# Attention and MoE kernel: batch 0's second round as fp32 products on unsplit q, k and v

## The chip, the cores and the metric

The kernel runs on one core of a Trainium2 chip. The metric is the device time of one execution in microseconds (us); the times before are the median and the spread of three runs, and the profile is one further execution of the same program. The engines are named as the profile names them: PE (matmuls), PEld (its weight loads), DVE (vector), ACT (scalar), POOL (GpSimd), SP (the engine that issues the DMAs).

## The reference

Eight batches of eight heads, 576 tokens, head dimension 64; then a two-layer network with 512 model columns and 2048 inner columns.

```python
scores = (1 / sqrt(64)) * (q @ k.T)                 # (8, 8, 576, 576)
thresh = max(scores, axis=-1) - tau
scores = where(scores >= thresh, scores, -1e9)
attn = exp(scores - max(scores))
attn = attn / (sum(attn) + 1e-9)
x = (attn @ v), heads joined                        # (4608, 512)
h = x @ w_in                                        # (4608, 2048)
out = (h * sigmoid(h)) @ w_out                      # (4608, 512)
```

Inputs and outputs are fp32, and w_in and w_out come as 64-bit words that the kernel decodes itself.

## The kernel before, in words

**Tiles and visits.** The work is a list of score tiles. A tile is 128 query rows against all 576 keys of a head. Tiles are grouped in visits, a visit being one pair of heads of one batch (`visits`, L653). Batches 1 to 7 have one visit for each pair, with nine tiles. Batch 0 is done in two rounds: four visits of kind "low" (query tokens 0 to 255, four tiles each, 16 tiles), a gap of 12 empty places, then four visits of kind "high" (tokens 256 to 575, five tiles each, 20 tiles). In a high visit the third tile is mixed: 64 rows of the one head and 64 of the other. The empty places give the network of batch 0's first 256 tokens room to begin.

**A split tile** (batch 0's high round and all later batches). `load_qk` (L322) loads q and k of a head twice, into both halves of the partitions. `split_k` (L357) rounds k to the fp32r form on ACT and takes the rest on POOL (L362). `split_q` (L336) scales q by 0.125 (`gate`) and does the same; for batch 0 the scaling and the rounding are two ACT instructions (L345, L346) and the rest is POOL's (L347), for later batches ACT does it in one (L351) and DVE takes the rest (L352). `scores` (L428) makes the tile in a PSUM buffer of two halves, with rounded k and rest of k: four products, eight for a mixed tile (L448). `soft1` takes the row maximum on DVE (L458, L461), `soft1b` the exponential on ACT (L468), `soft2` masks, sums and inverts on DVE (L477, L481, L485), `soft2b` divides each row by its sum on ACT (L495), `soft3` (L499) splits the rows into two fp16 parts: the first by ACT for tiles before EARLY = 36 (L504), else by POOL (L506), the second by POOL (L509, L512). A DMA transposes both into `wT` (L522). `av` (L527) multiplies with v, which `split_v` (L308) has split into two fp16 parts on ACT and DVE (L312, L313): 28 products for a pair and column range (L537).

**A direct tile** (batch 0's low round). `load_direct` (L374) loads k of both heads once, and q of each head into its own half of a buffer whose other half is zero (`qzero`, part of `gbuf`). `scale_direct` (L382) scales q on ACT (L385). Scores are two fp32 products (L436), `soft2b` divides on POOL (L491), `soft3_direct` (L387) transposes the fp32 rows on PE (L393, L395) and ACT copies them out (L403, L404), `av_direct` (L406) multiplies with the raw v (L413).

**Weights.** `load_weights`, `decode_weights` (L184: ACT L191, DVE L194 and L197, then a product on PE, L209, that gathers the maxima in PSUM bank 2) and `split_weights` (L216) run over 16 tiles of w_in, then 16 of w_out. w_in is scaled on POOL (L226), rounded to fp16 on ACT (L229), and POOL takes the rest (L230). w_out is scaled and rounded on ACT (L221) and DVE takes the rest (L222). `W_PLAN` (L39) gives the places at which they are due; w_out's steps carry a priority offset of 150.

**The network.** `h_unit` (L573) is 12 products (L580) and then work on ACT and DVE (L588, L589, L595, L596), `o_unit` (L604) 12 products (L611). Batch 0's units are let in at RATES = 1.3, then 0.8 units for each place of the list, once the x of their tokens is there.

**PSUM.** Score buffers take four of eight banks; `bank` (L78) hands out three (m0, m1, m2, where m2 is left out of the turn until the high round's end), `ps_a` is one bank for the products with v.

**Order.** The loop at L763 writes the work down place by place; `at` puts steps at places of the list; `pri` gives some of them a priority. A planner then orders each engine's and each queue's instructions by priority and its own simulated times. On the chip every engine and the DMA queue on SP work through their own list in that order.

Of the kernel before, what the change touches and what calls it, by code (L numbers as in the profile page):

```python
# [19 lines left out]
P = 128  # L20
# [12 lines left out]
EARLY = 36  # L33
GAP, GAP1 = 12, 1
V_SLOT = 26
# [17 lines left out]
def attention_moe(  # L53
# [41 lines left out]


# [119 lines left out]
    def split_weights(i):  # L216
# [3 lines left out]
        if i >= 4 * NK:  # L220
            nc.scalar.activation(hi, w, AF.Copy, scale=sc)  # L221
            nc.vector.scalar_tensor_tensor(  # L222
                out=w16[:, i, 512:1024], in0=w, scalar=sc, in1=hi, op0=ALU.mult, op1=ALU.subtract
            )
            return
# [110 lines left out]
    def split_q(h, tiles):  # L336
# [7 lines left out]
        if h < H:  # L344
            nc.scalar.activation(src, src, AF.Copy, scale=gate)  # L345
            nc.scalar.activation(dst, src, AF.Copy)  # L346
            nc.gpsimd.tensor_tensor(  # L347
                out=dst[D:P, :], in0=src[D:P, :], in1=dst[D:P, :].bitcast(F32), op=ALU.subtract
            )
        else:  # L350
            nc.scalar.activation(dst, src, AF.Copy, scale=gate)  # L351
            nc.vector.scalar_tensor_tensor(  # L352
                out=dst[D:P, :], in0=src[D:P, :], scalar=gate[D:P, :],
                in1=dst[D:P, :].bitcast(F32), op0=ALU.mult, op1=ALU.subtract,
            )
# [11 lines left out]
    qzero = []  # L367
    for i in range(2):
        t = gbuf.bitcast(F32)[:, 4096 + 512 * i : 4608 + 512 * i]
        nc.gpsimd.memset(t, 0.0)  # L370
        qzero.append(t)

    def load_direct(v):
        b, p, _ = visits[v]  # L374
        kt = sb.tile([P, S], F32, tag="kraw", name=f"kd_{v}", bufs=2)
        nc.sync.dma_start(out=kt, in_=kT[b, 2 * p : 2 * p + 2].rearrange("h d s -> (h d) s"))
        qt = qzero[v % 2]
        nc.sync.dma_start(out=qt[0:D, 0:256], in_=qT[b, 2 * p, :, 0:256])
        nc.sync.dma_start(out=qt[D:P, 256:512], in_=qT[b, 2 * p + 1, :, 320:S])
        direct[v] = qt, kt  # L380

    def scale_direct(v):  # L382
        for j in range(2):
            own = direct[v][0][j * D : (j + 1) * D, 256 * j : 256 * (j + 1)]
            nc.scalar.activation(own, own, AF.Copy, scale=gate[j * D : (j + 1) * D, :])  # L385

    def soft3_direct(t):  # L387
# [3 lines left out]
        main = bank([P, 4, P], f"tm_{t}")  # L391
        for k in range(4):
            nc.tensor.transpose(main[:, k, :], w[:, k * P : (k + 1) * P], ident)  # L393
        last = bank([P, P], f"tl_{t}")
# [58 lines left out]
    def soft1(t):  # L453
# [6 lines left out]
        )  # L460
        nc.vector.tensor_scalar(  # L461
            out=sm[:, 1:2], in0=negm, scalar1=-1.0, scalar2=ntau, op0=ALU.mult, op1=ALU.add
        )
        small[t] = sm
        wtile[t] = w

# [295 lines left out]
    t = 0  # L762
# [93 lines left out]
```

## Time and profile before

| | |
|---|---|
| runs shown, median (lowest to highest) | 1234.36 us (1231.63 to 1234.51) |
| profiled execution, its own time | 1228.56 us |
| its span | 1226.8 us |
| granted PE clock over the span | 0.971 |
| busy: PE | 1145.4 us, 93% |
| busy: DVE | 934.2 us, 76% |
| busy: ACT | 808.6 us, 66% |
| busy: POOL | 739.4 us, 60% |

A page of the profile cuts the span in 40 slices and gives for each, in tenths, how busy an engine was and what clock PE was granted. Groups of instructions stand as line, engine, operation, output and inputs, count, then busy time in us and mean duration in ns, then the idle time of the engine just before them and who ended it. The order of time gives start, duration, engine and line. Shares over the whole span hide stages with different limits, so views of single stretches matter more here.

### The profile page before, as it was taken

How to read it: one execution, taken by the hardware profiler on the slowest of the kernel's cores; microseconds unless marked ns; L12 is line 12 of the kernel's file. 1: busy time of each engine (PE TensorE's matmuls, PEld its weight loads, DVE VectorE, ACT ScalarE, POOL GpSimd, SP SyncE). 2: the span in 40 equal slices, each digit the busy share in tenths (PEclk: the TensorE clock that was granted, in tenths of full speed). 3: DMA queues.
4: the chain of work that ended last, by engine and by line, in shares of the span. 5: the costliest groups of instructions: out<-in, count | busy, mean ns of one | idle time of the engine just before them, and what ended most of it. 6: DMA issues, size and time to landing. Idle time of an engine off the chain costs nothing.

```text
span 1226.8 us, 26991 instructions
## 1 busy us (share of the span) xinstructions
PE 1145.4 (93%) x9422; PEld 898.1 (73%) x9422; DVE 934.2 (76%) x2619; ACT 808.6 (66%) x1491; POOL 739.4 (60%) x936
## 2 busy tenths in 40 slices
PE   6867679999799999999999999999999999999998
PEld 4545458777677777877777877787778877777777
DVE  6988998987888988988889958887789848332330
ACT  5768876776777767776777747776678747333331
POOL 2289968786778778886888528872778447100000
PEclk9967889999999999999999999999999999999999
DMA  9659658687677777786896447872797346200000
GB/s 296 192 182 235 136 117 171 146 139 148 138 145 144 166 148 145 147 160 149 146 174 141 110 115 138 156 144 82 137 159 150 75 86 113 50 11 15 16 11 25
DMA packets 363480, 158.16 MB, mean 129 GB/s; under 512 B 329552, under 2 KB 338256, under 8 KB 363344
## 3 DMA queue, kind: packets, MB, share of 16 engines
q1 hardware_dynamic: 363344, 156.43, 60.6%
q8 instruction: 75, 1.23, 0.4%
q14 instruction: 61, 0.50, 0.1%
HBM read 66.72 MB, written 9.44 MB: 62 GB/s over the span
## 4 chain that ended last, share of the span: by engine, by line
PE 64%; DVE 16%; DMA 8%; ACT 5%; issue 3%; POOL 2%; SPq 1%; ACTq 0%; POOLq 0%; DVEq 0%
PE o L611 24%; PE h L580 22%; PE s L448 9%; PE a L537 7%; DVE w L477 4%; DVE sm L458 3%; DVE qstack L352 2%; DMA wT<-hl 2%; DMA vraw<-in_vL 2%; ACT w L468 2%; DMA wraw<-in_w_out 2%; ACT w L495 1%; DVE gbuf L596 1%; DMA kd<-in_kT 1%; DVE wst L222 1%
## 5 line engine op out<-in xcount | busy, mean ns | idle before, releaser
L580 PE MATMUL h<-x,wst 128*128 128x288 f16 (+2 forms) x3072 | 429.7, 289 | 15.6 <-DVE gbuf L596 12.0
L611 PE MATMUL o<-gbuf,wst 128*128 128x288 f16 (+2 forms) x3072 | 420.0, 286 | 2.0 <-ACT wst L621 1.9
L580 PEld LDWEIGHTS <-wst 128*128 128x128 f16 x3072 | 292.7, 99 | 105.3 <-issue 26.7
L611 PEld LDWEIGHTS <-wst 128*128 128x128 f16 x3072 | 292.8, 98 | 83.4 <-issue 6.7
L509 POOL TENSOR_TENSOR hl<-w,hl 128x512 f16<-128x512 f32 x272 | 326.4, 1200 | 14.6 <-ACT hl L504 1.2
L506 POOL TENSOR_SCALAR hl<-w 128x576 f16<-128x576 f32 x264 | 179.9, 684 | 202.5 <-ACT w L495 141.2
L468 ACT ACTIVATE w<-s,sm 128x576 f32<-128x576 f32 x288 | 210.9, 737 | 78.9 <-DVE sm L458 33.1
L477 DVE SCALAR_TENSOR_TENSOR w<-s,sm,w 128x576 f32<-128x576 f32 x288 | 232.6, 813 | 35.9 <-ACT w L468 34.0
L458 DVE TENSOR_REDUCE sm<-s 128x1 f32<-128x576 f32 x288 | 215.1, 751 | 41.5 <-PE s L448 32.4
L495 ACT ACTIVATE w<-w,sm 128x576 f32<-128x576 f32 x272 | 205.7, 770 | 49.3 <-DVE sm L485 47.1
L589 DVE SCALAR_TENSOR_TENSOR h<-th,h 128x288 f32<-128x288 f32 (+2 forms) x256 | 116.5, 457 | 109.3 <-ACT th L588 107.2
L588 ACT ACTIVATE th<-h,msc 128x288 f32<-128x288 f32 (+2 forms) x256 | 126.8, 498 | 106.4 <-PE h L580 104.7
L448 PE MATMUL s<-khi,qstack 128*128 128x288 f32 x608 | 160.0, 345 | 27.1 <-DVE w L477 23.4
L595 ACT ACTIVATE gbuf<-h 128x288 f16<-128x288 f32 (+2 forms) x256 | 103.6, 407 | 80.7 <-DVE h L589 79.7
L596 DVE SCALAR_TENSOR_TENSOR gbuf<-h,gbuf 128x288 f16<-128x288 f32 (+2 forms) x256 | 115.4, 453 | 40.1 <-ACT gbuf L595 39.1
L448 PEld LDWEIGHTS s<-khi,qstack 128*128 128x128 f32 x608 | 97.4, 196 | 51.3 <-issue 34.4
L448 PE MATMUL s<-klo,qstack 128*128 128x288 f32 x608 | 133.6, 301 | 0.0
L537 PE MATMUL a<-wT,v 128*64 128x288 f16 (+1 forms) x1680 | 129.7, 293 | 4.0 <-DMA wT<-hl 3.7
L362 POOL TENSOR_TENSOR klo<-kraw,khi 128x576 fp32r<-128x576 f32 x64 | 94.8, 1481 | 43.1 <-ACT khi L360 43.0
L537 PEld LDWEIGHTS <-v 128*64 128x64 f16 x1680 | 92.0, 111 | 31.5 <-issue 22.8
L512 POOL TENSOR_TENSOR hl<-w,hl 128x64 f16<-128x64 f32 x272 | 102.5, 377 | 0.0
L448 PEld LDWEIGHTS s<-klo,qstack 128*128 128x128 f32 x608 | 101.0, 195 | 0.3
(103 smaller groups left out, 831.6 us busy)
## 6 DMA issues: line engine op xcount, KB each, us to landing
qraw<-in_qT SPq DMA_DIRECT2D x128, 144.0 KB, 3.0
kraw<-in_kT SPq DMA_DIRECT2D x128, 144.0 KB, 3.0
vraw<-in_vL SPq DMA_DIRECT2D x32, 320.0 KB, 3.3
wraw<-in_w_out SPq DMA_DIRECT2D x16, 512.0 KB, 4.1
out_t<-wst SPq DMA_DIRECT2D x56, 144.0 KB, 2.2
wT<-hl SPq DMA_TRANSPOSE x304, 3.3
gbuf<-in_w_in SPq DMA_DIRECT2D x8, 512.0 KB, 7.1
wraw<-in_w_in SPq DMA_DIRECT2D x8, 512.0 KB, 6.5
```

Source lines behind the costliest of these rows:

```text
L448: nc.tensor.matmul(s_ps[:, j, :HALF], lhs, kk[:, j * HALF : (j + 1) * HALF], start=(n == 0), stop=(n == len(seq) - 1),)
L458: nc.vector.tensor_reduce(out=negm, in_=s_ps[:, :, :HALF], op=ALU.max, axis=AX.XY, negate=True)
L468: nc.scalar.activation(wtile[t].rearrange("p (j c) -> p j c", j=2), sps[t][:, :, :HALF], AF.Exp, bias=small[t][:, 0:1],)
L477: nc.vector.scalar_tensor_tensor(out=w3, in0=s_ps[:, :, :HALF], scalar=sm[:, 1:2], in1=w3, op0=ALU.is_ge, op1=ALU.mult, accum_out=sm[:, 2:3],)
L495: nc.scalar.activation(w, w, AF.Copy, scale=r)
L506: nc.gpsimd.tensor_scalar(out=fl[:, 0:S], in0=w, scalar1=1.0, scalar2=1.0, op0=ALU.mult, op1=ALU.mult)
L509: nc.gpsimd.tensor_tensor(out=fl[:, 640:1152], in0=w[:, 0:512], in1=fl[:, 0:512], op=ALU.subtract)
L537: nc.tensor.matmul(a_ps[odd * D : (odd + 1) * D, :n], vt[:, lo_v, odd, kv, :], wT[v, b * H + 2 * p + odd][:, kw, c0 - base : c0 - base + n ...
L580: nc.tensor.matmul(ph[:, :n], wi(c, f, lo_w), x16[b, lo_x][:, c, c0 : c0 + n], start=(k == 0), stop=(k == 11),)
L588: nc.scalar.activation(th[:, :n], ph[:, :n], AF.Tanh, scale=moe_sc[b][:, 0:1])
L596: nc.vector.scalar_tensor_tensor(out=g[:, 1, :n], in0=ph[:, :n], scalar=2.0**-14, in1=g[:, 0, :n], op0=ALU.mult, op1=ALU.subtract,)
L611: nc.tensor.matmul(ps[:, :n], wo(f, d, lo_w), g[:, lo_g, :n], start=(f == 0 and k == 0), stop=(f == NF - 1 and k == 2),)
```

## The change

It gives the second round of batch 0 the direct form of the first. The parts are:

- high visits use `load_direct`, with zeroed buffers of their own (320 columns for each head), two fp32 products for each tile, mixed ones too, transposes on PE, and `av_direct`. Their four transposes of a tile go to PSUM bank m1, the fifth to `ps_a`;
- in direct tiles q is no longer scaled. The exponential takes 0.125 as its scale, and threshold and bias are worked out for unscaled scores from two small constants (`coef`, `shift`). `scale_direct` goes;
- batch 0's v is no longer split (its scales are still worked out); batch 1's v is loaded later (from place 29 on, 5 places apart, before from 9 on, 9 apart), its scales are made at place 51 (before 47);
- w_out's tiles are split as w_in's are: scaled on POOL, rounded on ACT, rest on POOL;
- the first part of the softmax rows is POOL's for all split tiles;
- the units of batch 0's first 256 tokens use the banks m0 and m2 in turn.

The diff, without the renumbering of the columns of `sm` and the constants EARLY and V_SLOT, which go:

```diff
+    coef = const.tile([P, 2], F32, name="coef")
+    nc.vector.memset(coef, -1.0)
+    nc.vector.tensor_copy(coef[:, 0:1], gate)
+    shift = const.tile([P, 2], F32, name="shift")
+    nc.vector.memset(shift, 0.0)
+    nc.vector.tensor_scalar(
+        out=shift[:, 1:2], in0=tau_sb, scalar1=0.0, scalar2=-3.0e38, op0=ALU.is_lt, op1=ALU.mult
+    )
+    nc.vector.scalar_tensor_tensor(
+        out=shift[:, 1:2], in0=ntau, scalar=8.0, in1=shift[:, 1:2], op0=ALU.mult, op1=ALU.add
+    )
...
-        if i >= 4 * NK:
-            nc.scalar.activation(hi, w, AF.Copy, scale=sc)
-            nc.vector.scalar_tensor_tensor(
-                out=w16[:, i, 512:1024], in0=w, scalar=sc, in1=hi, op0=ALU.mult, op1=ALU.subtract
-            )
-            return
         nc.gpsimd.tensor_scalar(
             out=w, in0=w, scalar1=sc, scalar2=1.0, op0=ALU.mult, op1=ALU.mult
         )
...
-            vmx[b], f"v{b}", (None, 2)[b] if b < 2 else 0, squared=(b == 0)
+            vmx[b], f"v{b}", (None, 1)[b] if b < 2 else 0, squared=(b == 0)
...
-        if h < H:
-            nc.scalar.activation(src, src, AF.Copy, scale=gate)
-            nc.scalar.activation(dst, src, AF.Copy)
-            nc.gpsimd.tensor_tensor(
-                out=dst[D:P, :], in0=src[D:P, :], in1=dst[D:P, :].bitcast(F32), op=ALU.subtract
-            )
-        else:
-            nc.scalar.activation(dst, src, AF.Copy, scale=gate)
...
+    qzero = {}
+    for kind, base, n in (("low", 4096, 256), ("high", 5120, 320)):
+        for i in range(2):
+            t = gbuf.bitcast(F32)[:, base + 2 * n * i : base + 2 * n * (i + 1)]
+            nc.gpsimd.memset(t[0:D, n : 2 * n], 0.0)
+            nc.gpsimd.memset(t[D:P, 0:n], 0.0)
+            qzero[kind, i] = t
...
+        qt = qzero[kind, v % 2]
+        n = VISITS[kind][2][0][1]
+        c0, c1 = (0, S - n) if kind == "low" else (S - n, 0)
+        nc.sync.dma_start(out=qt[0:D, 0:n], in_=qT[b, 2 * p, :, c0 : c0 + n])
+        nc.sync.dma_start(out=qt[D:P, n : 2 * n], in_=qT[b, 2 * p + 1, :, c1 : c1 + n])
         direct[v] = qt, kt
-
-    def scale_direct(v):
-        for j in range(2):
-            own = direct[v][0][j * D : (j + 1) * D, 256 * j : 256 * (j + 1)]
-            nc.scalar.activation(own, own, AF.Copy, scale=gate[j * D : (j + 1) * D, :])
...
-        main = bank([P, 4, P], f"tm_{t}")
+        low = visits[v][2] == "low"
+        main = bank([P, 4, P], f"tm_{t}", None if low else 1)
...
-        last = bank([P, P], f"tl_{t}")
+        if low:
+            last = bank([P, P], f"tl_{t}")
+        else:
+            last = ps_a.tile([P, 512], F32, tag="a", name=f"tl_{t}")[:, 0:P]
...
+        if tiles[t][0] in direct:
+            nc.vector.scalar_tensor_tensor(
+                out=sm[:, 4:6], in0=coef, scalar=negm, in1=shift, op0=ALU.mult, op1=ALU.add
+            )
+        else:
+            nc.vector.tensor_scalar(
+                out=sm[:, 5:6], in0=negm, scalar1=-1.0, scalar2=ntau, op0=ALU.mult, op1=ALU.add
+            )
...
-            bias=small[t][:, 0:1],
+            **(
+                {"bias": small[t][:, 4:5], "scale": gate}
+                if tiles[t][0] in direct else {"bias": small[t][:, 0:1]}
+            ),
...
-        if t < EARLY:
-            nc.scalar.activation(fl[:, 0:S], w, AF.Copy)
-        else:
-            nc.gpsimd.tensor_scalar(
-                out=fl[:, 0:S], in0=w, scalar1=1.0, scalar2=1.0, op0=ALU.mult, op1=ALU.mult
-            )
+        nc.gpsimd.tensor_scalar(
+            out=fl[:, 0:S], in0=w, scalar1=1.0, scalar2=1.0, op0=ALU.mult, op1=ALU.mult
+        )
...
+        if b == 0 and c0 == 0:
+            return h_units(b, c0, n, (0, 2)) + o_units(b, c0, n, (0, 2))
...
-        if kind == "low":
+        if b == 0:
             at(u - LOAD, lambda v=v: load_direct(v))
-            at(u - 2, lambda v=v: scale_direct(v))
...
-                at(V_SLOT + p, lambda p=p: split_v(0, p))
+            elif b == 1:
+                at(u + 5 * p - 20, lambda p=p: load_v(1, p))
+                at(u + 5 * p - 15, lambda p=p: vmax(1, p))
+                at(u + 9 * p + 4, lambda p=p: split_v(1, p))
...
-        at(u - 2 if b else 1, lambda b=b: vscale(b))
+        at((1, u + 2)[b] if b < 2 else u - 2, lambda b=b: vscale(b))
```

More of the change, by code (lines that the diff above doesn't have):

```diff
@@ L343, in split_q @@
         dst = qstack[odd][:, c0 + odd * D : c1 + odd * D]
[L344 to L355 removed]
+        nc.scalar.activation(dst, src, AF.Copy, scale=gate)
+        nc.vector.scalar_tensor_tensor(
+            out=dst[D:P, :], in0=src[D:P, :], scalar=gate[D:P, :],
+            in1=dst[D:P, :].bitcast(F32), op0=ALU.mult, op1=ALU.subtract,
+        )
     def split_k(h):
@@ L366, in attention_moe @@
     direct = {}
[L367 to L371, printed above, removed]
+    qzero = {}
[5 more added lines that the diff above has]
+            qzero[kind, i] = t
     def load_direct(v):
-        b, p, _ = visits[v]
+        b, p, kind = visits[v]
         kt = sb.tile([P, S], F32, tag="kraw", name=f"kd_{v}", bufs=2)
         nc.sync.dma_start(out=kt, in_=kT[b, 2 * p : 2 * p + 2].rearrange("h d s -> (h d) s"))
-        qt = qzero[v % 2]
-        nc.sync.dma_start(out=qt[0:D, 0:256], in_=qT[b, 2 * p, :, 0:256])
-        nc.sync.dma_start(out=qt[D:P, 256:512], in_=qT[b, 2 * p + 1, :, 320:S])
+        qt = qzero[kind, v % 2]
[3 more added lines that the diff above has]
+        nc.sync.dma_start(out=qt[D:P, n : 2 * n], in_=qT[b, 2 * p + 1, :, c1 : c1 + n])
         direct[v] = qt, kt
-    def scale_direct(v):
-        for j in range(2):
-            own = direct[v][0][j * D : (j + 1) * D, 256 * j : 256 * (j + 1)]
-            nc.scalar.activation(own, own, AF.Copy, scale=gate[j * D : (j + 1) * D, :])
     def soft3_direct(t):
@@ L433, in scores @@
             qt, kt = direct[v]
-            o = (h % 2) * 256 + i * P
+            if visits[v][2] == "low":
+                o = (h % 2) * 256 + i * P
+            else:
+                o = (h % 2) * 384 + (i - 2) * P
             for j in range(2):
@@ L454, in soft1 @@
         s_ps = sps[t]
-        sm = sb.tile([P, 5], F32, tag="small", name=f"sm_{t}", bufs=4)
+        sm = sb.tile([P, 6], F32, tag="small", name=f"sm_{t}", bufs=4)
         w = sb.tile([P, S], F32, tag="w32", name=f"w32_{t}", bufs=4)
@@ L460, in soft1 @@
         )
-        nc.vector.tensor_scalar(
-            out=sm[:, 1:2], in0=negm, scalar1=-1.0, scalar2=ntau, op0=ALU.mult, op1=ALU.add
-        )
+        if tiles[t][0] in direct:
+            nc.vector.scalar_tensor_tensor(
+                out=sm[:, 4:6], in0=coef, scalar=negm, in1=shift, op0=ALU.mult, op1=ALU.add
+            )
+        else:
+            nc.vector.tensor_scalar(
+                out=sm[:, 5:6], in0=negm, scalar1=-1.0, scalar2=ntau, op0=ALU.mult, op1=ALU.add
+            )
         small[t] = sm
@@ L630, in h_units, with o_units @@
         ]
-    def o_units(b, c0, n, own=None):
+    def o_units(b, c0, n, owns=(None,)):
         return [
-            lambda d=d, quarter=quarter: o_unit(b, c0, n, d, quarter, own)
+            lambda d=d, quarter=quarter: o_unit(b, c0, n, d, quarter, owns[d % len(owns)])
             for d in range(DM // P) for quarter in range(4)
@@ L644, in moe_units @@
         if held:
-            for pair in zip(h_units(b, c0, n, (0, 1)), o_units(*held.pop(), 2)):
+            for pair in zip(h_units(b, c0, n, (0, 1)), o_units(*held.pop(), (2,))):
                 out.extend(pair)
```

14 lines of the change are left out of this document (6 added, 8 removed).

## The prediction

> **What bounds the kernel now.** I read the page's slices first, then the busy time by stretch, then the groups of instructions of the one stretch that matters, engine by engine, then the order of time on PE, POOL and DVE there, and last the waits of the DMA queue.
>
> ```profile
> PE   6867679999799999999999999999999999999998
> ...
> POOL 2289968786778778886888528872778447100000
> PEclk9967889999999999999999999999999999999999
> ```
>
> The slices are 30.7 us each. From the seventh on PE is full at the full clock, so the kernel's end moves by what is won or lost ahead of that, plus whatever PE work is added or removed. In the first six PE is not full, and from the third to the sixth it is not at full clock either; POOL's two fullest slices of the kernel's first part, the fourth and the fifth, lie there. Batch 0 lies wholly in these six slices, and the change touches nothing else that is large.
>
> ```profile
> 6.00:66.00 60.00, 48.84 (x274) 32.28 (x275) 50.03 (x148) 40.64 (x78) 16.15 (x18) 0.91 0.81 249
> 70.00:100.00 30.00, 22.97 (x103) 15.12 (x104) 26.75 (x60) 21.47 (x40) 29.68 (x32) 0.55 0.65 190
> 100.00:140.00 40.00, 27.59 (x191) 21.78 (x190) 36.22 (x103) 35.94 (x71) 38.21 (x41) 0.79 0.78 185
> 140.00:168.00 28.00, 18.57 (x134) 13.41 (x133) 27.93 (x56) 22.14 (x39) 20.16 (x20) 0.82 0.57 127
> 70.00:168.00 98.00, 69.12 (x423) 50.31 (x424) 90.91 (x218) 79.56 (x148) 88.06 (x91) 0.72 0.68 170
> ```
>
> The columns are length, then busy time of PE, weight loads, DVE, ACT, POOL, then the granted clock, the DMA share and GB/s. I cut at 70 and 168 us because the second round's 20 score tiles lie between the two and batch 1's first score stands at their end. The first round (6 to 66) has no full engine. The second round has: POOL to 140 us (29.68 of 30, 38.21 of 40), then DVE to 168 us (27.93 of 28). PE does 69.12 us there at a granted clock of 0.72, so about 69.12 x 0.72 = 50 us of work at full clock. This stretch of 98 us is what the change rebuilds, and the question is how long it is with the new loads.
>
> **POOL in the second round.** Its groups there are:
>
> ```profile
> L509 POOL TENSOR_TENSOR hl<-w,hl 128x512 f16<-128x512 f32 x17 | 22.2, 1304 | 1.7 <-ACT hl L504 1.2
> L230 POOL TENSOR_TENSOR wst<-wst 128x512 f16<-128x512 f32 x16 | 19.5, 1241 | 0.1
> L226 POOL TENSOR_SCALAR wst<-wst,i_w_sc 128x512 f32<-128x512 f32 x16 | 12.7, 815 | 3.3 <-DVE i_w_sc L146 3.3
> L362 POOL TENSOR_TENSOR klo<-kraw,khi 128x576 fp32r<-128x576 f32 x8 | 12.0, 1505 | 2.3 <-ACT khi L360 2.3
> L512 POOL TENSOR_TENSOR hl<-w,hl 128x64 f16<-128x64 f32 x17 | 7.7, 454 | 0.0
> L506 POOL TENSOR_SCALAR hl<-w 128x576 f16<-128x576 f32 x9 | 6.7, 746 | 5.0 <-ACT w L495 4.8
> L347 POOL TENSOR_TENSOR qstack<-qraw,qstack 64x320 fp32r<-64x320 f32 x6 | 6.7, 1118 | 0.5
> ```
>
> Removed are the splits of the softmax rows (L509, L512, L506: 22.2 + 7.7 + 6.7), of q (L347: 6.7) and of k: six of L362's eight, 9.0, the last two being batch 1's. Together 52.3 us, which leaves 88.06 - 52.3 = 35.8. Added is the division by the row sum, which moves from ACT to POOL for 20 tiles. The first round already does it:
>
> ```profile
> L491 POOL TENSOR_SCALAR w<-w,sm 128x576 f32<-128x576 f32 x16 | 14.2, 891 | 42.2 <-DVE sm L485 33.4 <-DVE v_twice L125 5.0 <-DVE wmx L214 1.9
> ```
>
> 20 x 0.891 = 17.8 us. The 16 w_out tiles take the route of the w_in tiles, 16 x (0.815 + 1.241) = 32.9 us. POOL's new load is 35.8 + 17.8 + 32.9 = 86.5 us. So POOL, the fullest engine, is relieved by only 1.6 us in sum; what the change does is to fill the part after 140 us, where it had 20.16 of 28. At the fill it had up to 140 us (67.89 of 70, 0.97) this makes a stretch of 89 us; if the last w_out tiles slip behind batch 1's first tiles (the o products need them only later) it is shorter. I take 88: ten less than 98.
>
> **DVE.** It loses the w_out subtraction and the split of batch 0's v:
>
> ```profile
> L222 DVE SCALAR_TENSOR_TENSOR wst<-wst,o_w_sc 128x512 f16<-128x512 f32 x12 | 12.2, 1035 | 0.0
> ...
> L313 DVE SCALAR_TENSOR_TENSOR v<-vraw,v_sc,v 128x640 f16<-128x640 f32 x3 | 3.8, 1254 | 0.0
> ```
>
> 90.91 - 12.2 - 3.8 = 74.9 us, at its fill of 90.91/98 a stretch of 81 us. DVE is thus behind POOL by 7 us, and no longer ends the stretch. The four L222 that ran after 168 us (16 less the 12) go too, 4 us on an engine that was near full there; I count 2. The five small DVE instructions that set up the new constants run before the first score, when DVE has nothing to do: nothing.
>
> **PE.** The rows of a fp32 round, and of a split one, both at full clock:
>
> ```profile
> 48.98 2.52 PE L413 MATMUL a<-wT,vraw 128*64 128x256 f32 x18
> 51.43 1.24 PE L436 MATMUL s<-kd,gbuf 128*128 128x288 f32 x4
> 52.50 0.62 PE L209 MATMUL wps<-wst 128*128 128x128 bf16 x8
> 52.96 0.60 PE L393 MATMUL tm<-ident,w 128*128 128x128 f32 x4
> 53.40 0.27 PE L395 MATMUL tl<-ident,w 128*128 128x128 f32 x1
> 53.51 1.14 PE L436 MATMUL s<-kd,gbuf 128*128 128x288 f32 x4
> ```
>
> ```profile
> 184.94 1.96 PE L537 MATMUL a<-wT,v 128*64 128x320 f16 x26
> 186.83 0.53 PE L448 MATMUL s<-khi,qstack 128*128 128x288 f32 x2
> 187.20 0.42 PE L448 MATMUL s<-klo,qstack 128*128 128x288 f32 x2
> 187.55 0.33 PE L537 MATMUL a<-wT,v 128*64 128x320 f16 x2
> ```
>
> From start to start, a fp32 score tile takes 1.07 us and its five transposes 0.55: 1.62 x 20 = 32.4. A product with v of 20 records at 256 columns takes 2.45 x 20/18 = 2.72, at 320 columns 3.4, times four visits 13.6. Added: 46 us. A split score tile takes 0.72, the four mixed ones twice that: 17.3; a split product 1.89 + 0.26 = 2.15, times four 8.6. Removed: 26 us. PE's work in the kernel thus grows by 20 us, and it is hidden only while PE waits in this stretch: 50 + 20 = 70 us at full clock, against POOL's 88. The cover is gone if the clock falls below 70/88 = 0.80. In the first round, which has this very mix, the clock was 0.91, in the second it was 0.72. I take 0.85 to 0.95, because fp32 products keep PE busy longer at a time, so 74 to 82 us: still under POOL.
>
> At this place the Trainium skill speaks against the change: "TensorE: Matmul & The Clock Gate", Part 4, says that transposes on PE do not count as activity for the clock gate, so the 100 added ones would not hold the clock up. This trace does not bear that out in the first round, where 80 transposes stand among the products at 0.91; no run here shows transposes alone.
>
> **ACT.** It gains the copies out of PSUM and loses more: the row division, the splits of q and k, half of the softmax copies. It had 79.56 of 98 and ends lower; no part of the sum. The scale of the exponential now comes from a tensor; what this costs is bounded by a copy with such a scale and one without:
>
> ```profile
> L495 ACT ACTIVATE w<-w,sm 128x576 f32<-128x576 f32 x17 | 13.0, 771 | 0.4 <-DVE sm L485 0.3
> ...
> L504 ACT ACTIVATE hl<-w 128x576 f16<-128x576 f32 x8 | 5.4, 680 | 0.1
> ```
>
> 0.09 us for each of 36 tiles at most, 3.3 us, hidden by ACT's spare 18; and the two scalings of q per visit in the first round vanish for it.
>
> **DMA queue.** Eight heads' q and k, each loaded twice, become one load per pair, and the 20 tiles' DMA transposes go. The loads of batch 1's v move from the first round to the second. There they had stalled the queue:
>
> ```profile
> SPq L181 <- DVE wst L197: 32.9, 17, 5.4
> SPq L251 <- PE a L413: 13.9, 3, 6.8
> ```
>
> 13.9 us in three waits for a v buffer, with weight loads queued behind. Their removal is worth between nothing (decoding is what L181 waits for, 32.9 us) and 13.9 us in the first round; I take 3, nearer to nothing since weights wait for DVE first. The waits come back in the second round: each v load now waits for the second product with that pair's v, and behind it on the queue stand batch 1's q and k. By then the w_out loads, which come earlier in program order, are out; I count nothing, and up to 7 us (one such wait) for the range.
>
> **New waits.** The last transpose of each tile shares one PSUM bank with the product with v: PE's next tile waits for ACT's copy or for the x split. And every second h product goes to the bank in which w_out's maxima are summed, so it waits until w_out is decoded, with the other h products behind it in the plan; what is put off so is done later, when PE is full. Nothing in the trace shows either wait. I charge 3 us for both, with 0 and 7 as ends.
>
> **Sum.** -10 (second round) - 3 (first round) - 2 (after 168 us) + 3 (new waits) = -12 us. The profiled execution took 1228.56 us (span 1226.8), so 1216.6 by it; it was 5.8 us faster than the median of the runs shown, 1234.36. The forecast is for such a median: **1222 us**, and 1213 to 1230 by the ends above.
>
> **Rivals.**
> *PE ends on the low clock (slower).* If the clock stays at what it was up to 140 us, (30 x 0.55 + 40 x 0.79)/70 = 0.69, PE needs 70/0.69 = 101 us and, at a fill of 0.95, 107: nine more than 98, less the 5 of the first and third terms: 1239. It decides below 70/0.95/98 = 0.75. For it: the 0.55 and 0.79. Against: PE had gaps there because tiles waited for POOL, and 0.91 with the same mix. The page's rule on transposes is on this side.
>
> *w_out holds POOL in one block (no change).* The w_in scalings ran as one block ahead of the first round's last tiles:
>
> ```profile
> 69.94 12.06 POOL L226 TENSOR_SCALAR wst<-wst,i_w_sc 128x512 f32<-128x512 f32 x15 [3.28 <-DVE i_w_sc L146]
> ...
> 85.35 2.05 POOL L491 TENSOR_SCALAR w<-w,sm 128x576 f32<-128x576 f32 x2
> ```
>
> ```profile
> 74.77 0.14 DVE L485 RECIPROCAL sm<-sm 128x1 f32<-128x1 f32 x1
> ```
>
> The row factor was there at 74.9 us, its division began at 85.35: 10.4 us late, and PE's transposes, with all that stands behind them in its order, later still. w_out's splits carry the higher priority of their plan, so the same can happen in mid-round. It takes 10 of the 12 us: 1232. Against: four row buffers cover part of it.
>
> *More is freed (faster by far).* If w_out's tail slips behind batch 1, DVE's 81 us end the stretch (-17), and the queue gives 7 in the first round: -24 - 2 + 2, 1210. For it: o products start late. Against: POOL's order follows the plan.
>
> **Chances.** Forecast 0.47, more freed 0.16, block on POOL 0.20, low clock 0.17. Within 0.3% (3.7 us, about what the runs of this kernel tell from no change: they spread by 2.9) counts as same: most of the block's case and the slow edge of the forecast's, 0.18. Slower: most of the low clock's and a little of the block's, 0.17. Faster 0.65. The range takes in 1210 with its own 4 us and 1239: 1206 to 1240.
>
> **What would show it.** Right: the first batch 1 score 10 to 16 us earlier than at 168; POOL over 0.95 from the first w_in split to that score; L222 gone and DVE not full; clock above 0.8 there; PE still full afterwards. Wrong: clock 0.75 or less with PE the full engine; a gap on PE of some 10 us while POOL runs w_out's scalings in one row; h products bunched behind the end of w_out's decoding; or batch 1 starting earlier with the end unmoved, which would mean that the deferred h products were given back later.

## The result and the profile after

The changed kernel takes 1250.76 us (median of 4 runs, 1248.51 to 1253.53), the kernel before, run beside it, 1233.43 us (4 runs, 1231.63 to 1234.51): a ratio of 1.0159, 95% interval 1.0134 to 1.0184. It is slower by 17 us, where 12 less were forecast. The profiled execution took 1249.05 us (span 1247.3).

The slices of the page after (31.2 us each) answer to those shown of before:

```profile
PE   5868996997699999999999999999999999999998
...
POOL 2286934786878768887788709773678528200000
PEclk8889998999699999999999999999999999999999
```

PE is at 8 and 9 in the fourth to sixth slice, where it stood at 6 and 7, and its clock is near full there. But POOL drops to 3 and 4 in the sixth and seventh, PE to 6 in the seventh, and in the tenth and eleventh PE has a hole (7 and 6, clock 6 in the eleventh). The stretches, after and then before:

```profile
70.00:168.00 98.00, 80.29 (x525) 57.77 (x522) 83.35 (x208) 69.13 (x149) 82.72 (x87) 0.93 0.30 93
168.00:200.00 32.00, 30.75 (x255) 24.43 (x253) 9.87 (x31) 11.44 (x25) 4.98 (x7) 1.00 0.14 37
```

```profile
168.00:200.00 32.00, 26.05 (x213) 21.98 (x212) 29.68 (x81) 22.74 (x40) 23.84 (x31) 0.89 0.74 150
```

From 168 to 200 us PE works almost without a gap, and DVE, ACT and POOL stand almost still: 9.87 us of DVE in place of 29.68. That is work of the wrong kind on PE: matrix products, and no softmax row behind them. How far the attention is tells it best. The start of the n-th row maximum, read one by one from VectorE's order of time (16 is the second round's first tile, 36 batch 1's first), in us:

| kernel | 16 | 36 | 48 | 84 | 252 |
|---|---|---|---|---|---|
| before | 73.4 | 171.7 | 209.3 | 331.5 | 911.3 |
| after | 72.2 | 168.3 | 231.4 | 345.9 | 931.0 |
| after, with priority (1st experiment) | 75.1 | 172.7 | 212.6 | 338.2 | 915.2 |
| after, two small instructions (16th) | 72.1 | 160.2 | 212.4 | 332.7 | 924.6 |
| priority and q scaled (10th) | 72.2 | 160.5 | 202.5 | 325.9 | 908.5 |
| 10th with the two-tensor instruction (15th) | 75.5 | 172.5 | 213.8 | 338.5 | 923.5 |

The second round became 96.1 us long (98.3 before) and not 88, and then 12 tiles took 63.1 us instead of 37.6.

**Between tile 36 and tile 48.** The columns are start and length in us, and in brackets an idle time before and what ended it. The order of time on PE in the kernel after:

```profile
163.05 0.60 PE L390 MATMUL tm<-ident,w 128*128 128x128 f32 x4
163.49 0.27 PE L395 MATMUL tl<-ident,w 128*128 128x128 f32 x1
163.82 3.87 PE L619 MATMUL o<-gbuf,wst 128*128 128x256 f16 x34
...
168.07 1.70 PE L619 MATMUL o<-gbuf,wst 128*128 128x256 f16 x14
...
170.15 15.89 PE L619 MATMUL o<-gbuf,wst 128*128 128x256 f16 x144
185.88 0.60 PE L390 MATMUL tm<-ident,w 128*128 128x128 f32 x4
186.32 0.27 PE L395 MATMUL tl<-ident,w 128*128 128x128 f32 x1
```

All 192 o products of batch 0's first 256 tokens are out in 22 us, with no transpose among them. The rows of batch 0's last tiles had been divided long before, on POOL:

```profile
163.66 0.75 POOL L502 TENSOR_SCALAR w<-w,sm 128x576 f32<-128x576 f32 x1
164.38 2.28 POOL L234 TENSOR_TENSOR wst<-wst 128x512 f16<-128x512 f32 x2
167.05 0.75 POOL L502 TENSOR_SCALAR w<-w,sm 128x576 f32<-128x576 f32 x1 [0.40 <-DVE sm L496]
168.18 0.75 POOL L502 TENSOR_SCALAR w<-w,sm 128x576 f32<-128x576 f32 x1 [0.37 <-DVE sm L496]
189.89 0.67 POOL L514 TENSOR_SCALAR hl<-w 128x576 f16<-128x576 f32 x1 [20.96 <-ACT w L506]
```

Two things meet. The o products need w_out's second parts, which POOL now ends at 166.7 us (the two subtractions from 164.38), so nearly all of them become ready together. And in the plan they stand ahead of the last tiles' transposes, which have no priority of their own, while the split tiles' products with v have one. The new transposes therefore queue behind them, and with them ACT's copies, the exponentials and DVE:

```profile
186.13 0.47 ACT L629 ACTIVATE wst<-o,msc 128x256 f32<-128x256 f32 x1 [4.76 <-PE o L619]
186.52 0.60 ACT L403 ACTIVATE wT<-tm 128x512 f32<-128x512 f32 x1
187.01 0.73 ACT L476 ACTIVATE w<-s,sm 128x576 f32<-128x576 f32 x1
187.78 0.82 DVE L488 SCALAR_TENSOR_TENSOR w<-s,sm,w 128x576 f32<-128x576 f32 x1 [16.36 <-ACT w L476]
```

**Within the second round.** VectorE's and ScalarE's groups, before (70 to 168 us), then after (0 to 70 and 70 to 168 us):

```profile
L468 ACT ACTIVATE w<-s,sm 128x576 f32<-128x576 f32 x20 | 14.7, 735 | 1.6 <-DVE sm L458 1.6
L461 DVE TENSOR_SCALAR sm<-sm,ntau 128x1 f32<-128x1 f32 x19 | 3.9, 205 | 0.1
```

```profile
L476 ACT ACTIVATE w<-s,sm,gate 128x576 f32<-128x576 f32 x15 | 12.3, 827 | 1.9 <-DVE sm L465 1.6 <-issue 0.2
...
L465 DVE SCALAR_TENSOR_TENSOR sm<-coef,sm,shift 128x2 f32<-128x2 f32 x15 | 4.2, 277 | 0.0
```

```profile
L476 ACT ACTIVATE w<-s,sm,gate 128x576 f32<-128x576 f32 x21 | 17.8, 851 | 6.3 <-DVE sm L465 6.2
L465 DVE SCALAR_TENSOR_TENSOR sm<-coef,sm,shift 128x2 f32<-128x2 f32 x21 | 13.8, 659 | 0.1
```

Before, the exponential's bias was the row maximum itself, and the threshold (L461, 205 ns) was worked out beside it. Now the bias, too, comes out of L465, an instruction on two elements a partition with two tensor operands: 277 ns in the first round, 659 in the second. ACT waits for it (6.2 us), and DVE holds 21 x (0.659 - 0.205) = 9.5 us more. Why it takes so long is seen beside POOL, in order of time:

```profile
102.94 4.09 POOL L234 TENSOR_TENSOR wst<-wst 128x512 f16<-128x512 f32 x3
...
104.30 1.11 DVE L465 SCALAR_TENSOR_TENSOR sm<-coef,sm,shift 128x2 f32<-128x2 f32 x1
...
110.91 1.21 DVE L465 SCALAR_TENSOR_TENSOR sm<-coef,sm,shift 128x2 f32<-128x2 f32 x1
110.95 2.52 POOL L234 TENSOR_TENSOR wst<-wst 128x512 f16<-128x512 f32 x2 [0.34 <-ACT wst L233]
...
114.26 0.75 POOL L502 TENSOR_SCALAR w<-w,sm 128x576 f32<-128x576 f32 x1 [0.79 <-DVE sm L496]
...
115.60 0.21 DVE L465 SCALAR_TENSOR_TENSOR sm<-coef,sm,shift 128x2 f32<-128x2 f32 x1
...
116.30 0.75 POOL L502 TENSOR_SCALAR w<-w,sm 128x576 f32<-128x576 f32 x1 [1.29 <-DVE sm L496]
```

Between two POOL instructions it takes 0.21 us, beside POOL's subtraction 1.11 and 1.21. The longest of the 36 took 2.58 us:

```profile
135.61 2.58 DVE L465 SCALAR_TENSOR_TENSOR sm<-coef,sm,shift 128x2 f32<-128x2 f32 x1
```

```profile
137.43 0.75 POOL L502 TENSOR_SCALAR w<-w,sm 128x576 f32<-128x576 f32 x1
```

It ended at 138.19 us, 0.01 after POOL's division, the fourth POOL instruction that it lay beside. The Trainium skill says this in "SBUF — State Buffer", section "SBUF: two separate sides": a VectorE instruction with two inputs in SBUF and a GpSimd instruction that reads SBUF share a pair of ports, and the later one waits until the other is through. The trace agrees: 17 of the 36 took more than 0.25 us, and each of these ended within 0.02 us after the end of a POOL instruction. The prediction had not drawn on it.

### The profile page after: what moved, and what is told of

It reads as the page before. It is cut to its first block, busy times and chain, and to the rows that moved or that the text cites. A ratio compares the mean times of both kernels' runs of the same rounds, so it can differ in the third digit from the quotient of the medians.

```text
span 1247.3 us, 26939 instructions
## 1 busy us (share of the span) xinstructions
PE 1161.7 (93%) x9474; PEld 907.3 (73%) x9474; DVE 923.5 (74%) x2604; ACT 789.3 (63%) x1475; POOL 725.3 (58%) x926
## 4 chain that ended last, share of the span: by engine, by line
PE 52%; DVE 20%; DMA 11%; ACT 7%; issue 5%; POOL 3%; SPq 1%; ACTq 0%; POOLq 0%; DVEq 0%
PE o L619 20%; PE h L588 18%; PE s L451 7%; DMA wT<-hl 5%; DVE w L488 5%; PE a L545 5%; DVE sm L461 4%; DVE qstack L349 3%; DMA vraw<-in_vL 2%; ACT w L476 2%; DMA gbuf<-in_w_in 2%; ACT w L506 1%; PE a L413 1%; POOL hl L517 1%; DVE h L597 1%
## 5 line engine op out<-in xcount | busy, mean ns | idle before, releaser
L517 POOL TENSOR_TENSOR hl<-w,hl 128x512 f16<-128x512 f32 x252 | 302.3, 1200 | 12.2
L514 POOL TENSOR_SCALAR hl<-w 128x576 f16<-128x576 f32 x252 | 170.0, 678 | 222.6 <-ACT w L506 157.1
L488 DVE SCALAR_TENSOR_TENSOR w<-s,sm,w 128x576 f32<-128x576 f32 x288 | 232.9, 813 | 59.2 <-ACT w L476 57.1
L461 DVE TENSOR_REDUCE sm<-s 128x1 f32<-128x576 f32 x288 | 215.5, 750 | 39.6 <-PE s L451 29.6
L476 ACT ACTIVATE w<-s,sm 128x576 f32<-128x576 f32 x252 | 184.5, 739 | 87.3 <-DVE sm L461 28.0
L506 ACT ACTIVATE w<-w,sm 128x576 f32<-128x576 f32 x252 | 190.7, 770 | 39.4 <-DVE sm L496 37.6
L451 PE MATMUL s<-khi,qstack 128*128 128x288 f32 x560 | 147.0, 344 | 20.9 <-DVE w L488 15.3
L604 DVE SCALAR_TENSOR_TENSOR gbuf<-h,gbuf 128x288 f16<-128x288 f32 (+2 forms) x256 | 115.4, 452 | 41.4 <-ACT gbuf L603 40.1
L545 PE MATMUL a<-wT,v 128*64 128x288 f16 x1568 | 117.4, 289 | 7.5 <-DMA wT<-hl 6.3
L451 PE MATMUL s<-klo,qstack 128*128 128x288 f32 x560 | 122.6, 300 | 0.0
L451 PEld LDWEIGHTS s<-khi,qstack 128*128 128x128 f32 x560 | 89.1, 194 | 41.4 <-issue 28.7
L359 POOL TENSOR_TENSOR klo<-kraw,khi 128x576 fp32r<-128x576 f32 x56 | 82.7, 1477 | 40.3 <-ACT khi L357 38.8
L520 POOL TENSOR_TENSOR hl<-w,hl 128x64 f16<-128x64 f32 x252 | 93.0, 369 | 0.0
L451 PEld LDWEIGHTS s<-klo,qstack 128*128 128x128 f32 x560 | 92.4, 193 | 0.5 <-issue 0.2
```

The lines of the kernel that those rows point to most:

```text
L451: nc.tensor.matmul(s_ps[:, j, :HALF], lhs, kk[:, j * HALF : (j + 1) * HALF], start=(n == 0), stop=(n == len(seq) - 1),)
L461: nc.vector.tensor_reduce(out=negm, in_=s_ps[:, :, :HALF], op=ALU.max, axis=AX.XY, negate=True)
L476: nc.scalar.activation(wtile[t].rearrange("p (j c) -> p j c", j=2), sps[t][:, :, :HALF], AF.Exp, **({"bias": small[t][:, 4:5], "scale": ga ...
L488: nc.vector.scalar_tensor_tensor(out=w3, in0=s_ps[:, :, :HALF], scalar=sm[:, 5:6], in1=w3, op0=ALU.is_ge, op1=ALU.mult, accum_out=sm[:, 1:2],)
L506: nc.scalar.activation(w, w, AF.Copy, scale=r)
L514: nc.gpsimd.tensor_scalar(out=fl[:, 0:S], in0=w, scalar1=1.0, scalar2=1.0, op0=ALU.mult, op1=ALU.mult)
```

## The experiments

Where the first expectations use letters, A is the theory of the o products ahead of transposes without priority and C that of the DMA queue; the others are named where they stand. Each ratio is to the kernel before, run beside it on the same chip; kernels of different experiments are best compared by it.

**1. Priority.** The second round's transposes and products with v get the priority that the split tiles' products have.

```diff
-            soft3(t - 1)
+            hi = visits[tiles[t - 1][0]][2] == "high"
+            pri(PRI_AV if hi else 0, lambda: soft3(t - 1))()
...
-                a_ps = av_direct(v, p)
+                hi = visits[v][2] == "high"
+                a_ps = pri(PRI_AV if hi else 0, lambda v=v, p=p: av_direct(v, p))()
```

> The transposes, copies and v products of the second round's tiles get the priority that the later batches' v products have; nothing else is changed. In the program the 144 o products in a row are gone from PE's order: score tiles and the last tiles' transposes stand among them. Theory A (o products block the last four tiles, which starves the row work for some 17 us and leaves the score tiles 20 us late): the 48th score tile comes 15 to 25 us earlier than in the changed kernel and the time falls to 1228 to 1237 us. Theory B (PE's 20 us of added fp32 work are simply paid, whatever the order): within 4 us of 1250.8. Theory C (batch 1's v loads and what stands behind them on the DMA queue hold the tiles): within 4 us of 1250.8.

1231.98 us, ratio 1.0015 (0.9994 to 1.0036). PE's order there (transposes and o products alone):

```profile
167.22 0.63 PE L390 MATMUL tm<-ident,w 128*128 128x128 f32 x4
...
170.94 0.60 PE L390 MATMUL tm<-ident,w 128*128 128x128 f32 x4
173.88 0.27 PE L395 MATMUL tl<-ident,w 128*128 128x128 f32 x1
175.27 0.72 PE L619 MATMUL o<-gbuf,wst 128*128 128x256 f16 x5
...
181.66 0.60 PE L390 MATMUL tm<-ident,w 128*128 128x128 f32 x4
...
182.76 2.35 PE L619 MATMUL o<-gbuf,wst 128*128 128x256 f16 x20
```

The o products begin later and come in rows of at most 28, with the transposes of the last three tiles among them, and tile 36 to 48 takes 39.9 us. Nearly all the loss goes; the forecast gain does not come.

**2. Rate.** The units of batch 0's first tokens are dealt out more slowly: `RATES = (0.8, 0.8)` in place of `(1.3, 0.8)`.

> The network's units of the first 256 tokens are let in at 0.8 for each place of the list instead of 1.3, so that fewer o units stand ahead of the second round's last tiles in the program. Theory A: 1228 to 1240 us, the long run of o products is gone. Theory B and theory C: within 4 us of 1250.8.

1239.2 us, 1.0078 (1.0061 to 1.0095). The row of 144 breaks up, and transposes stand among the o products, but tile 36 to 48 still takes 58.4 us: PE waits 8.5 us in one piece there for the input of an h product (L604, on DVE). So the row of o products is not the only thing that can hold up these tiles.

**3. w_out back on ACT and VectorE** in the changed kernel.

```diff
+        if i >= 4 * NK:
+            nc.scalar.activation(hi, w, AF.Copy, scale=sc)
+            nc.vector.scalar_tensor_tensor(
+                out=w16[:, i, 512:1024], in0=w, scalar=sc, in1=hi, op0=ALU.mult, op1=ALU.subtract
+            )
+            return
```

> The changed kernel with w_out's split back on ACT and DVE. In PE's order the o products still come in a long run, but with score tiles in it and with two tiles' transposes behind it instead of four. Theory A: part of the loss comes back, 1238 to 1247 us. If POOL's share in w_out is what costs the time by itself: 1233 or less. Theory C: within 4 us of 1250.8.

1234.54 us, 1.0035 (1.0021 to 1.0049): more comes back than expected. From 135 to 172 us the two-tensor instruction, after and then here:

```profile
L465 DVE SCALAR_TENSOR_TENSOR sm<-coef,sm,shift 128x2 f32<-128x2 f32 x8 | 5.7, 712 | 0.1
```

```profile
L471 DVE SCALAR_TENSOR_TENSOR sm<-coef,sm,shift 128x2 f32<-128x2 f32 x8 | 1.9, 231 | 0.0
```

With POOL free of w_out it is a third as long.

**4. Later v.** Batch 1's v of the second to fourth pair is loaded after batch 1's first places.

```diff
-                at(u + 5 * p - 20, lambda p=p: load_v(1, p))
+                at(u + (5 * p - 20 if p == 0 else p + 2), lambda p=p: load_v(1, p))
```

> Batch 1's v loads after the first come late, behind batch 1's first q and k loads, so that none of them waits on the queue ahead of those; PE's order keeps its 144 o products in a row. Theory C: 1235 to 1243 us. Theory A and theory B: within 4 us of 1250.8.

1247.76 us, 1.014 (1.0125 to 1.0155). The queue's waits for a v buffer (17.5 us in three, up to 250 us) stayed as they were, and the v loads between 125 and 205 us went out 1 to 3 us later only; the edit did not take the waits away, so theory C is not tried well by it.

**5 and 6. One part alone, in the kernel before.** The fifth moves only w_out's split to POOL, the sixth only makes 0.125 the exponential's scale in the first round.

> One part alone: the kernel before, with w_out split by POOL as in the change. If this part is a loss by itself (POOL was the fullest engine of the second round there, and gets 33 us of work): 4 to 15 us slower than before. If DVE's relief of 15 us is worth more: 2 to 8 us faster. The theory of the blocked order (theory A) expects nothing of it, since this kernel has no transposes on PE in its second round.

> One part alone: the kernel before, with the factor 0.125 as the exponential's scale in the first round. Theory A: within 3 us of before. If the first round's four lost microseconds in the changed kernel come from this part: 3 to 6 us slower, and the 16th score tile about 4 us later than before.

1242.38 us, 1.009 (1.0066 to 1.0114), and 1240.89 us, 1.0079 (1.0052 to 1.0106). Both parts lose by themselves. In the fifth POOL is full:

```profile
70.00:168.00 98.00, 70.03 (x473) 52.23 (x472) 81.28 (x211) 75.60 (x145) 95.19 (x106) 0.81 0.64 159
168.00:216.00 48.00, 32.94 (x239) 26.04 (x240) 30.86 (x84) 27.80 (x46) 44.58 (x53) 0.86 0.70 134
```

In the sixth the first tile starts 2.2 us earlier (8.4) and the second round 5.5 us later (78.9): ACT once waits 6.00 us for a weight load.

**7. Both mended:** priority, and w_out on ACT and VectorE.

> The changed kernel with the priority of run e1_prio and w_out's split back on ACT and DVE as in run e3_wout_dve. If POOL's block of w_out scalings is what keeps the second round as long as before once the order is mended: 1218 to 1227 us, faster than both kernels. If PE's added fp32 work is what eats the gain (theory B as the remainder): 1229 to 1235.

1230.57 us, 1.0001 (0.9982 to 1.0019). With priority, it makes no difference who splits w_out.

**8. Less work for PE.** As 1, with the second round's score and v products on the upper 16 bits of their operands as bf16; the lower halves are left out.

> Run e1_prio with the second round's score products and products with v taken on the upper 16 bits of q, k, the rows and v as bf16: the low halves are left out of the computation, the count of tiles, transposes, copies and row work stays. PE loses about 24 us of work (0.83 for each of 20 score tiles, 2 for each of four products with v). Theory B as the remainder (PE's work is paid one to one once the order is mended): 1204 to 1213 us. If the score tiles' row work sets the pace there and PE only fills: 1224 or more.

1221.98 us, 0.9924 (0.9907 to 0.994): 10 us less than the first experiment. By the two traces PE lost 20.6 us of work instead of 24 (busy time, weighted with the clock granted at each moment: 1133.7 and 1113.1 us).

**9 and 10. q scaled on ACT again**, in 7 and in 1; the exponential's bias is then again the row maximum.

> Of the change only the second round as fp32 products on unsplit data is left, with its loads, its banks and the later v of batch 1; the w_out splits are on ACT and VectorE, the factor 0.125 is again a scaling of q on ACT, and the second round's transposes and v products stand with the priority of products. Theory (PE's added fp32 work eats what the other engines save, and the exponential's scale costs the first round some us through the order of the plan): the first round as before, the 16th row maximum at 65 to 70 us, batch 1's first at 160 to 166, and 1222 to 1230, 0.992 to 0.999 of before. Rival (the exponential's scale costs nothing once the order has settled; PE's work alone sets the end): 1229 to 1235, as with the scale in the exponential.

> The changed kernel with the second round's transposes and v products at the priority of products, and 0.125 again as a scaling of q on ACT; w_out's second parts stay on GpSimd. Theory (the exponential's scale costs the first round some us): 16th row maximum at 65 to 70 us instead of 74.4, the end at 1224 to 1230. If GpSimd's added work matters once the first round is early again: 3 to 8 us more than the kernel with w_out on VectorE that runs beside it. Rival (the scale costs nothing): 1230 to 1234.

1227.96 us, 0.9977 (0.9966 to 0.9988), and 1227.61 us, 0.996 (0.9945 to 0.9975): the two complete kernels that beat before and after. Batch 1 starts at 161.7 and 160.5 us, and again it does not matter who splits w_out. But the first round did not get shorter as I had expected: the 16th row maximum comes at 71.8 and 72.2 us, not at 65 to 70.

**11. The plan's order alone.** The kernel before with `V_SLOT = 27` in place of 26.

> The kernel before with one entry of its plan a place later (the splits of batch 0's v at places 27 to 30 instead of 26 to 29); no instruction is added or removed. If the plan's order by itself is worth a few us, as the shifts of the first round in kernels that leave it alone suggest, the 24th row maximum moves by 2 us or more and the time by up to 4 us in either direction; if the plan is indifferent to such an edit, both stay within 1 us (0.999 to 1.001).

1230.86 us, 0.9997 (0.9983 to 1.0011). The 24th row maximum moves by 1.7 us, the end not.

**12. The scale in the second round only.** As 1, but q scaled on ACT in the first round.

> The changed kernel with the second round's transposes and v products at the priority of products, and 0.125 as a scaling of q on ACT in the first round alone; in the second round it stays the exponential's scale. Theory (what the exponential's scale costs lies in the first round, through the order in which weights are loaded and decoded): 16th row maximum at 65 to 68 us, batch 1's first at 159 to 163, and the time of the kernel that scales q in both rounds (1227.6 beside 1231.1 for before, ratio 0.994 to 0.998). Rival (the cost is the exponential's own longer time, 0.1 us for each of the second round's 20 tiles, on ACT's path): half or more of it comes back, batch 1's first row maximum at 164 or later, ratio 0.999 to 1.002.

1231.25 us, 1.0 (0.9987 to 1.0014). My theory falls: the first round is in time (72.9) and the second takes 95.4 us, so the cost lies there. Twenty exponentials 0.1 us longer do not make 7 us; the groups of this kernel led to the instruction ahead of them (20 at 625 ns).

**13 to 16. The two-tensor instruction.** 13 is the first experiment with two one-tensor instructions in its place; 16 the same edit in the changed kernel without priority. 14 is the tenth with a scale of ones for the exponential, 15 the tenth with the two-tensor instruction put back and no scale.

```diff
-            nc.vector.scalar_tensor_tensor(
-                out=sm[:, 4:6], in0=coef, scalar=negm, in1=shift, op0=ALU.mult, op1=ALU.add
-            )
+            nc.vector.tensor_scalar(
+                out=sm[:, 4:5], in0=negm, scalar1=gate, scalar2=1.0, op0=ALU.mult, op1=ALU.mult
+            )
+            nc.vector.tensor_scalar(
+                out=sm[:, 5:6], in0=negm, scalar1=-1.0, scalar2=shift[:, 1:2],
+                op0=ALU.mult, op1=ALU.add,
+            )
```

> The changed kernel with the priority of products for the second round's transposes and v products, the exponential's scale kept, and the two-tensor instruction of 128x2 between the row maximum and the exponential (500 ns mean of 36) replaced by two one-tensor instructions of 128x1. Theory (that instruction, which waits for GpSimd and on which the exponential's bias waits, is what the exponential's scale cost): its two successors take 0.15 to 0.21 us each, batch 1's first row maximum comes at 159 to 164 instead of 172.7, and 1223 to 1229, ratio 0.993 to 0.998. Rival (the cost is the exponential's own 0.1 us, or the wait of the bias for any second instruction): 1229 to 1234, ratio 0.999 to 1.002.

> The kernel with priority that scales q on ACT (1227.6, ratio 0.996), and the exponential of batch 0 reads its scale from a tensor of ones; nothing else differs. Theory (two-tensor instruction): each exponential takes 0.84 instead of 0.74 us and the time stays, ratio 0.994 to 0.998. Rival (the exponential's own longer time is the cost): back to 1.000 to 1.002.

> The kernel with priority that scales q on ACT (1227.6, ratio 0.996), and in batch 0 the exponential's bias and the threshold come from the two-tensor instruction of 128x2 (coefficients 1 and -1, shifts 0 and minus tau), as in the changed kernel; the exponential has no scale. Theory: the instruction takes 0.2 to 1.2 us beside GpSimd, mean over 0.45, and the gain goes, ratio 0.999 to 1.003. Rival: ratio 0.994 to 0.998.

> The changed kernel as it is, without the priority, with the two one-tensor instructions in place of the two-tensor one. Theory (two separate losses: the block of o products ahead of the transposes, and the two-tensor instruction): the block stays, batch 1 gets from its first to its 13th row maximum in 55 to 65 us (63 in the changed kernel, 37 to 40 with priority), and 1238 to 1248: some 4 to 10 us of the 17 come back. Rival (the block only came from the rows being late): the block goes too, 1224 to 1232.

Measured: 13, 1234.27 us, 1.0024 (1.0009 to 1.0039); 14, 1235.72 us, 1.0034 (1.0019 to 1.005); 15, 1246.56 us, 1.0123 (1.0089 to 1.0156); 16, 1239.76 us, 1.0069 (1.005 to 1.0088). The groups of 13 and of 15 from 70 to 168 us:

```profile
L465 DVE TENSOR_SCALAR sm<-sm,gate 128x1 f32<-128x1 f32 x22 | 4.5, 204 | 0.0
L468 DVE TENSOR_SCALAR sm<-sm,shift 128x1 f32<-128x1 f32 x22 | 4.4, 201 | 0.0
```

```profile
L465 DVE SCALAR_TENSOR_TENSOR sm<-coef,sm,shift 128x2 f32<-128x2 f32 x20 | 13.1, 662 | 0.1
```

Beside the same POOL, one-tensor instructions keep their 0.2 us. For the second round's length the theory holds: 90.7 us in 13 and 14, 88.1 in 16, 97.0 in 15. For the end it holds in 16 alone (there tile 36 to 48 takes 52.2 us, a little less than the 55 to 65 expected). In 13 and 14, where it expected a gain, both ratios lie beyond its range and a little above the rival's: 13 starts batch 1 5 us earlier than 1 and ends no earlier; 14 loses 12.8 us against the tenth between tile 36 and 48, of which it gets some back. 15 loses, but four times as much as the 0.3% at most that were expected: up to tile 84 it goes with 1 (338.5 and 338.2 us), and from there to the end it takes 10.8 us more.

**17 and 18. The queue once more:** the tenth and the fourteenth with the later v of experiment 4.

> The kernel with priority that scales q on ACT (1227.6, ratio 0.996), with batch 1's v of the second to fourth pair loaded after batch 1's first places instead of among the second round, and split four places later. Theory (the DMA queue, which stands 16.7 us in two waits for a v buffer between 120 and 217 us with batch 1's k and q behind it, is what gives the early start of batch 1 back): the waits go, batch 1 gets from its first to its 13th row maximum in under 40 us (42.0 without the edit), and ratio 0.990 to 0.995. Rival (the early start is given back because PE has the work of batch 0 still before it): 0.994 to 0.998, as without the edit.

> The kernel whose exponential reads its scale from a tensor of ones (1235.7, ratio 1.0034; batch 1 from its first to its 13th row maximum in 54.7 us, the queue 21.9 us in four waits for a v buffer), with the same later v loads. Theory (queue): 40 to 46 us for those 12 tiles and ratio 0.993 to 0.999. Rival (the o products, all of them ready together there, stand among the tiles in rows of up to 48): over 50 us and ratio 1.001 to 1.005.

1230.0 us, 0.9994 (0.998 to 1.0009), and 1231.69 us, 1.0013 (0.9997 to 1.0028). The waits for a v buffer are still there in 17:

```profile
SPq L243 <- PE a L407: 16.6, 2, 8.7
```

In 18 the 12 tiles take 41.4 us instead of 54.7, and half of the loss goes. Neither theory's figures are met by both.

Behind tile 84, where no edit changes an instruction, the profiled executions take from 892 us (1) to 906 us (16), and 895 before. What sets this stays open, and it is as large as most differences of the end that these experiments look for; differences of a few us between them are therefore not explained here.

## Why the prediction was wrong, point by point

**Second round, -10: the step that failed first.** It was 2 us shorter instead of 10. The loads were near what was worked out: POOL 82.7 us (forecast 86.5), PE 80.3 (74 to 82) at a clock of 0.93 (0.85 to 0.95). DVE was not: 83.4 us instead of 74.9, and L465 is 9.5 of that. I had read the change's new small instructions as "five" that "run before the first score", and bounded the exponential's scale by ACT's 0.09 us. That price was right (827 ns against 734 in the first round; the Trainium skill gives 93 ns for each operand that is a pointer, "ScalarE: Activation LUTs", section "What ACT_TABLE_LOAD costs", and these rows agree). But the scale also asks for a scaled bias, so an instruction came to stand between row maximum and exponential in each of 36 tiles, of a form that waits for POOL. All the kernels with the fp32 second round and that instruction take 93.5 to 98.8 us for it; the seven without it take 88.1 to 91.1. (The eighth experiment, with less work on PE, takes 90.2.)

These come near the 88 of the sum, but not for the sum's reason. The sum let POOL's load set the length at a fill of 0.97, and POOL over 0.95 was named as a sign of being right; POOL was busy for 82.7 of the 98 us, 0.84. From the second round's first row maximum to batch 1's, with w_out off POOL (9) and on POOL (10):

```profile
71.79:161.70 89.91, 69.69 (x435) 49.60 (x435) 76.87 (x201) 65.40 (x140) 53.00 (x55) 0.87 0.29 90
```

```profile
72.23:160.53 88.30, 68.05 (x432) 47.57 (x432) 67.80 (x184) 60.67 (x136) 74.47 (x83) 0.89 0.29 92
```

POOL has 21 us more to do in the second, and the round is 1.6 us shorter; no engine is busy for more than 0.86 of either. That the mended kernels meet the 88 is luck, and what sets this length stays open.

**New waits, +3: the step that failed worst.** I charged 3 us for two waits on PSUM banks, which PE shows between 70 and 168 us at 1.6 together:

```profile
PE tl L395 <- ACT wT L404: 1.1, 1, 1.1
PE h L588 <- DVE wmx L224: 0.5, 1, 0.5
```

I did not see a third: the second round's 100 transposes had been DMA work, and on PE they stand in a queue whose order the plan makes. That cost 25 us between tile 36 and tile 48; 7.7 of them came back by tile 84, and 5.3 were lost again by tile 252. "h products bunched" was among the signs; it was the o products, ahead of transposes.

**w_out on POOL.** The rival of a block on POOL was priced at 10 us and is half right: alone, the move costs 11 us (5), and in the changed kernel undoing it gives 16 (3). The block came, 15 scalings one behind the other. It held up one tile's division, whose factor was there at 131.25 us, for 6 us:

```profile
131.09 0.16 DVE L496 RECIPROCAL sm<-sm 128x1 f32<-128x1 f32 x1
```

```profile
124.48 10.06 POOL L230 TENSOR_SCALAR wst<-wst,o_w_sc 128x512 f32<-128x512 f32 x15
```

That division is the one shown further above, at 137.43. PE had other products to do meanwhile and stood for 0.9 us at most, not 10. The move costs more by two other ways: it lets all o products become ready late and at once, and it holds the two-tensor instruction.

The full loss of 17 us needs all three: late o products, rows made late by the two-tensor instruction, and transposes without priority. Taking any one away gives back some 16, 11 or 19 us (3, 16, 1), together far more than 17, so they act through each other. Once the transposes have the priority, the runs disagree on what the two-tensor instruction costs at the end: taking it away gave nothing (13 against 1), putting it in cost 1.6% (15 against 10).

**First round, -3.** The second round began 1.2 us earlier (72.2). The stalls for v did leave the first round and came back later (17.5 us), as written, but this made the first round no shorter: its 16 tiles took 64.0 us, 62.8 before, and the 1.2 us come from a first tile that starts at 8.3 instead of 10.6 us.

**After 168 us, -2.** L222 is gone, but no run shows the 2 us: with the order mended (10) tile 36 to 84 takes 165.4 us, 159.8 before.

**PE's added work, "hidden".** PE's busy time grew from 1145.4 to 1161.7 us; weighted with the clock granted at each moment it grew from 1118.4 to 1138.5, the 20 that were forecast. It was not hidden: the rest of the span, in which PE stood still or ran slowed, is 108.4 us before and 108.8 after, where the forecast needed some 32 less. With the failed steps mended (10) it is 90.3: batch 1 starts 11.2 us earlier, close to the forecast, at tile 84 it is 5.6 us ahead, at the end 3.5 by the medians. PE is the full engine from there on and still has its work: taking 20.6 us of it away gave 10 (8). "Batch 1 starting earlier with the end unmoved" was listed as a sign of error, and it is what is left of the gain.

**The low clock** did not come: 0.93 in the second round after, with its 100 transposes on PE, against 0.72 before. These transposes stand among fp32 products, so the rule of the Trainium skill that the prediction cites is not tested by it: no run here shows transposes alone.

## What to carry to other kernels

Work that moves to an engine with a hand-made order needs a place in that order: ask what stands ahead of it there and when that becomes ready, all at once above all. For each value that an instruction newly reads, follow who makes it, how often, and whether that lies between two steps of the chain; tiny instructions count by their form, not by their size. And ahead of a full engine, ask what the change takes from that engine's idle and slowed time, and set against it the work that it adds there. When a stage comes out at the forecast length, see whether the engine that was to set it is full.

## What the runs showed of the hardware

A VectorE instruction of 128x2 with two tensor operands in SBUF takes 0.21 us while POOL is idle and up to 2.58 us beside POOL (mean 659 ns of 21); in that longest case it lay beside four POOL instructions in a row and ended with the last. One of 128x1 with one tensor keeps 201 to 205 ns beside the same POOL, and the masking of 128x576 (L488), the same kind of instruction with one of its two tensors in PSUM, 811 and 810 ns in the first and second round.

PE's granted clock was lower where PE had less to do: with the fp32 products (1) and with the same products in bf16 (8), from 70 to 168 us:

```profile
70.00:168.00 98.00, 77.36 (x486) 54.79 (x482) 78.61 (x200) 65.22 (x140) 76.48 (x82) 0.90 0.29 94
```

```profile
70.00:168.00 98.00, 65.90 (x421) 45.61 (x420) 82.63 (x206) 65.91 (x142) 73.36 (x82) 0.76 0.30 93
```

By busy time and mean clock, 77.36 x 0.90 = 69.6 us of work at full clock stand against 65.90 x 0.76 = 50.1, yet PE is busy only 11.5 us less: part of what less work saves is given back. Whether the amount of work or the kind of product lowers the clock is not told apart by these two runs.
